# Delta-rule attention and a GELU MLP on one Trainium2 core: exponent activations parted, a join moved, unread products in other banks, masks earlier on GpSimd

## The chip, the cores and the metric

The kernel runs on one core of a Trainium2 chip. A core has five engines with a queue each, and each works through its own queue in order: TensorE (PE, with its weight loads shown as PEld), VectorE (DVE), ScalarE (ACT), GpSimd (POOL) and SyncE (SP, which here only starts transfers). They wait for one another through semaphores. The metric is the device time of one execution in microseconds (us), the median of several runs. A profiled execution also gives a trace, with the start and duration of every instruction; its times are those quoted below.

## The reference

Two parts, all in fp32. The first is attention by the delta rule, for 4 batches, 8 heads, 768 steps and a head size of 48; a 48x48 state is carried from step to step:

```python
k_n = k / (np.linalg.norm(k, axis=-1, keepdims=True) + 1e-06)
for t in range(S):
    kt, vt, bt = (k_n[:, :, t], v[:, :, t], beta[:, :, t, None])
    y[:, :, t] = np.einsum('bhd,bhde->bhe', q[:, :, t], state)
    v_old = np.einsum('bhde,bhd->bhe', state, kt)
    state = state + bt[:, :, :, None] * np.einsum('bhd,bhe->bhde', kt, vt - v_old)
```

Its result, with the heads side by side, is a matrix x of 3072 tokens by 384, which goes through a layer with GELU:

```python
h = x @ w_in                               # 384 -> 2048
g = 0.5 * h * (1.0 + erf(h * inv_sqrt2))
out = g @ w_out                            # 2048 -> 384
```

The weights w_in and w_out reach the chip as 64-bit floating-point words and are turned into fp32 there.

## The kernel before

**Tiling.** The 768 steps are cut into 12 chunks of 64, and the recurrence within a chunk becomes a triangular system that is solved at once. A unit is one chunk of a pair of batches, one batch on each half of the 128 partitions; there are two pairs, so two units to a chunk. Four units (chunks 0 and 1) form `first`: first[0], first[1] are chunk 0 (first[:NA], NA=2), first[2], first[3] are chunk 1.

**The triangular solve.** For a group of two chunks the systems are inverted in blocks of 32x32 by elimination (`eliminate_steps`): for each row j, one product into tmp (L558) and one sum into Nu (L560). In groups 0 and 1 these run on DVE, in later ones on GpSimd. The first group's rows are followed by ng, a factor made from the norms (L1344), and by two transpositions, Nu to XM (L569) and Nu to Zf (L572). Then the blocks are joined by products on TensorE. For chunk 0, `join_first(0)` does so by products psJ (L634), scaled into XM by DVE (L643) and ScalarE (L647), after GpSimd has scaled a block (L625); `join_first(1)` issues the second set (L634) and copies psJ on (L649). For chunk 1 it is `join`, whose level 0 ends in DVE products into XM (L613) and whose level 1 ends in copies on ScalarE (L617). `upper_left` makes two copies on ScalarE, one for each half (L586). `masked` multiplies the unit's products P by a triangular mask on GpSimd (L506); P is copied out of PSUM by ScalarE (L503). `scale_v` multiplies V by its norms on GpSimd (L421). `against_state` multiplies V of chunk 0 by ng, for first[0] on GpSimd (L783) and for first[1] on ScalarE, a head at a time (L780, 8 of them).

**The weights' decoding.** There are eight parts of w_in (`n` from 0 to 7) and then the parts of w_out. `fetch` starts a part's transfer on SP; `begin` takes the exponent bits out on DVE (L265 or L268); `exponents` turns them into a scale on ScalarE, by two Prelu for most parts (`two_kinks`; the calls are recorded at L1073 because they go through `keep`, which holds program order) or by one Relu (L271); `mantissas` makes the significand on DVE (L286, then L289); `signed` multiplies the two on DVE (L297, for some parts L296 before it) and then calls `fetch(n + 4)`, since the buffer of part n is free from there on.

**The layer.** Chunks 0 and 1 go through it by plain products, `fc1` (L976, with a GELU on ScalarE for each, recorded at L1073) and `fc2` (L991); from chunk 2 on it is by a scheme with seven products for eight (L1024, L1090).

**What sets the order.** Up to `by_hand.close()` the order of every engine's queue is that of the program, written out by hand. `unread` issues products of a blank tile whose results nobody reads; they go to the two PSUM banks of `sq`, which are used for other products too. `behind_rows` makes a step's first TensorE instruction wait for the latest DVE instruction in program order; `between` and `idle` say which steps follow which row. After that, `plan` is a list of steps with due times in units of a chunk, sorted by `emit`; DVE and GpSimd keep that order, and so do the calls of ScalarE and SP that go through `keep`. `decode_in` gives the due times of parts 3 to 7, and `behind_vector` makes a GpSimd step wait for the latest DVE instruction.

Of the kernel before, what the change touches and what calls it, by code (L numbers as in the profile page):

```python
# [8 lines left out]
F32 = mybir.dt.float32  # L9
U32 = mybir.dt.uint32  # L10
I32 = mybir.dt.int32
I16 = mybir.dt.int16
# [7 lines left out]
def kernel(  # L20
# [54 lines left out]
    def sq(name, *shape):  # L75
        return small[0].tile([128, *shape], F32, tag="sq", name=name)
# [179 lines left out]
    def high(e, dt):  # L256

        return e.bitcast(dt).rearrange("q (n w) -> q n w", w=2)[:, :, 1]
# [9 lines left out]
            nc.vector.tensor_scalar(e, raw[:, :, 1], 20, 0x7FF, op0=ALU.logical_shift_right,  # L268
                                    op1=ALU.bitwise_and)

    def exponents(n, put=lambda fn, *args, **kw: fn(*args, **kw)):  # L271
        e = halves[n][3]
        if two_kinks(n):
            f = e.bitcast(F32)
            put(nc.scalar.activation, f, e.bitcast(I32), ACT.Prelu, bias=lim[:, 2:3], scale=1.0,
                alpha=FLAT)
            put(nc.scalar.activation, high(e, I16), f, ACT.Prelu, bias=lim[:, 3:4], scale=128.0,
                alpha=1.0 / FLAT)
        else:
            put(nc.scalar.activation, e, e, ACT.Relu, bias=lim[:, 0:1], scale=float(2 ** 23))  # L280

# [33 lines left out]

    def decode_in():

        marks = {3: (None, 1.079, 0.99, 1.08), 4: (1.0, 1.113, 1.1, 1.13),
                 5: (1.12, 1.18, 1.14, 1.2), 6: (1.19, 1.24, 1.21, 1.25),
                 7: (1.245, 1.3, 1.29, 1.36)}  # L320
        steps = []
        for n, (a, b, c, d) in marks.items():
            if a is not None:
                steps += [(a, (begin, n))]
            steps += [(b, (exponents, n, keep)), (c, (mantissas, n)), (d, (signed, n))]
        return steps

    NW = len(w_parts)
# [176 lines left out]
    def masked(u, engine=nc.gpsimd):  # L505
        engine.tensor_tensor(u.P, u.P, mask_h, op=ALU.mult)  # L506
# [76 lines left out]
        steps += [(0.1, diagonal)]  # L583
        return steps + [(1.9, back, x) for x in range(3 if g else 2)]

    def upper_left(us, put=lambda fn, *args: fn(*args)):  # L586

        for p in range(2):
            top = slice(p * C, p * C + HB)
            put(nc.scalar.copy, Zf[0][top, us, 0:HB], Zf[0][top, us, HB:C])  # L590

# [178 lines left out]

    SIDES = [(0, 0), (1, 0), (0, 1), (1, 1)]

    def against_state(us):

        for u in us:
            u.W = u.V
            u.y = None
            if u.c == 0 and u.a:
                for h in range(H):
                    nc.scalar.mul(u.V[:, h], u.V[:, h], ng[:, u.a, h:h + 1])  # L780
                continue
            if u.c == 0:
                nc.gpsimd.tensor_tensor(u.W, u.V,  # L783
                                        ng[:, u.a].unsqueeze(2).to_broadcast([128, H, D]),
                                        op=ALU.mult)
                continue
            w = D if u.c == 1 else D + C
            psK = dn("psK")
            u.psK = psK[:, :, 0:NP * w].rearrange("q r (j d) -> q r j d", d=w)
            for j in range(NP):  # L790
                for r, p in QUADS:
                    rows = slice(r * C, r * C + D)
                    nc.tensor.matmul(u.psK[HALF[p], r, j, :], lhsT=u.Kt[rows, p, j, :],  # L793
                                     rhs=SQ[rows, u.a, p ^ r, j, 0:w], start=True, stop=True)
            if u.c == 1:
                u.psQ = psK[:, :, NP * D:2 * NP * D].rearrange("q r (j d) -> q r j d", d=D)
                against_queries([u])
        if us[0].c > 2:
            subtract(us)
# [438 lines left out]
    def at(first, last, steps):  # L1238

        total, done, timed = sum(s[0] for s in steps), 0.0, []  # L1240
        for w, *step in steps:
            timed.append((first + (last - first) * (done + 0.5 * w) / total, step))
            done += w
        return timed
# [11 lines left out]
            src = psB[HALF[p]].rearrange("q c (a p h) -> q c a p h", p=2, h=H)[:, :, :, p, :]  # L1256
            nc.scalar.mul(beta_m[HALF[p], c0:c1], src, -1.0)

    def unread(*cols):

        psI = sq("psI", 512)
        for n in cols:
            m = min(n, 128)
            nc.tensor.matmul(psI[0:m, 0:n], lhsT=blank[:, 0:m], rhs=blank[:, 0:n],
                             start=True, stop=True)
# [17 lines left out]
    n0 = wk.tile([128, 2 * NA, H], F32, tag="n0", name="n0", bufs=1)  # L1283
    for c in range(2):
        ns[c] = n0[:, c * NA:(c + 1) * NA]
    unread(512, 512)
    for u in first:
        squares(u, n0[:, u.t], nc.gpsimd if u.t == 1 else nc.vector)
        transposed(u, (0,))
# [27 lines left out]
    def latest(engine):  # L1317
        return next(i for i in reversed(nc.cur_bb.bb.instructions) if i.engine == engine)

    def behind_rows(fn, *args, engine=mybir.EngineType.PE):  # L1320

        after = latest(mybir.EngineType.DVE)
        n = len(nc.cur_bb.bb.instructions)
        fn(*args)
        new = next(i for i in nc.cur_bb.bb.instructions[n:] if i.engine == engine)
        tc.add_manual_dep(new, after.name,
                          mybir.DependencyInfo(mybir.DependencyClass.Sync,
                                               mybir.DependencyReason.DATA), reason="time")

    def turned(us, x):  # L1330
        for u in us:
            transposed(u, (x,))

    between = {9: [(turned, third, 0)], 10: [(grams, third)], 12: [(turned, third, 1)],
               15: [(turned, fourth, 0)], 17: [(grams, fourth)]}
    idle = {14: (256,), 18: (256,), 19: (256,), 20: (256,), 21: (256,), 22: (256,), 23: (256,), 24: (256,), 25: (256,), 28: (256,)}
    between.update({j: [(unread, *cols)] for j, cols in idle.items()})
    for fn, *args in rows:
        fn(*args)
        for step in between.get(args[0], ()) if args else ():  # L1340
# [1 line left out]
    for x in sums_:  # L1342
        sum_of_squares(*x)
    nc.vector.scalar_tensor_tensor(ng, gms[0][:, 0:NA], -1.0, ns[0], ALU.mult, ALU.mult)  # L1344
    behind_rows(unread, 512, 512)
    back0[0](*back0[1:])
    against_state(first[:NA])
    for u in first[:NA]:
        masked(u)
    back1[0](*back1[1:])  # L1350
    join_first(0)
    upper_left(slice(0, NA * H))
    after = latest(mybir.EngineType.PE)
    for n in range(n_in, n_in + 2):
# [3 lines left out]
                               if i.engine == mybir.EngineType.SP), after.name,  # L1358
                          mybir.DependencyInfo(mybir.DependencyClass.Sync,
                                               mybir.DependencyReason.DATA), reason="time")  # L1360
    unread(512, 256)
    begin(0)
    mantissas(0, (0,))
    join_first(1)
# [39 lines left out]
            steps = steps[:-1] + [(turn, tiles[c, a]) for a in range(NA)]  # L1404
        return [(t, step) for t, step in zip(times, steps) if t is not None]

    def behind_vector(fn, *args):
        behind_rows(fn, *args, engine=mybir.EngineType.Pool)

    plan = [at(c + 1 + 0.25 * (c == 1), c + 2 + 0.25 * (c == 0), ffn_steps(c)) for c in range(4)]  # L1410
    plan += [at(c + 1, c + 3, ffn_steps(c)) for c in range(4, NC, 2)]
    plan += [decode_in(), at(1.365, 1.9, decode_steps(n_in, NW)), at(1.91, 1.911, [(1.0, late)])]
    rows1, join1 = eliminate_steps(1), join_steps(1)
    plan += [at(1.1, 1.105, [(1.0, load, 3)]),
             at(1.112, 1.1121, [(1.0, upper_left, slice(NA * H, NU), keep)]),
             [(t, (together, (join, 0, range(NA, 2 * NA), level))) for level, t in enumerate((1.085, 1.16))],
]
    sums = [(1.0, sum_of_squares, tiles[3, a], h) for a in range(NA) for h in range(H)]
    plan += [at(1.48, 1.8, sums), at(1.81, 1.811, [(1.0, fn, c) for c in (2, 3) for fn in (norms, prep)]), at(1.9, 1.905, [(1.0, finish_both)]),
             *[at(t, t + 0.001, [(1.0, behind_vector, fn, u)]) for t, fn, u in (  # L1420
                 (1.201, scale_v, first[2]), (1.231, scale_v, first[3]),
                 (1.322, masked, first[2]), (1.37, masked, first[3]))],
             at(1.31, 1.311, [(1.0, together, (against_state, first[NA:]))]),
             at(1.325, 1.326, [(1.0, subtract, first[NA:])]),
             at(1.42, 1.421, [(1.0, together, (solve, first[NA:], ()))]),
# [144 lines left out]
```

## Time and profile before

| what | value |
|---|---|
| time, median of 3 runs | 621.89 us (621.54 to 622.21) |
| the profiled execution's own time | 623.14 us |
| its span | 621.4 us |
| mean granted clock of TensorE | 0.992 |
| PE busy | 606.9 us, 98% |
| DVE busy | 438.2 us, 71% |
| ACT busy | 246.2 us, 40% |
| POOL busy | 215.0 us, 35% |

The span runs from the first to the last recorded instruction; the execution's own time has what lies around it besides. Busy shares are means over the whole span. In the page's 40 slices (15.5 us each, tenths busy) the front differs from the rest:

```profile
PE   7899999999999999999999999999999999999997
DVE  7989999999867697765859656859646946422532
ACT  5777777624532265134452034452033322044200
POOL 6020232000479721786222885222885200000000
PEclk9889999999999999999999999999999999999999
```

TensorE's share includes the unread products of the first four slices. GpSimd is idle through most of the second and the fourth slice. PEclk is the clock that TensorE was granted, in tenths of full speed.

### The profile page before, as it was taken

To read this page: it belongs to the slowest core of one execution; us is meant where nothing else is said; L and a number is where in the kernel's file an instruction comes from. 1 tells how busy PE (TensorE), PEld (TensorE's weight loads), DVE (VectorE), ACT (ScalarE), POOL (GpSimd) and SP (SyncE) were. 2 spreads that over 40 slices of the span, in tenths; PEclk is the share of its full clock that TensorE was granted. 3 is DMA by queue.
4 is the path that set the end of the run, shared out by engine and by line. 5 is a ranking of instruction groups with operands and counts; after the bars stand their busy time and mean duration, and the time that the engine had idled before them with its cause. 6 is when DMAs were issued, how large, how long until landed. Compare 5 with 4: busy or idle time off the path is not lost.

```text
span 621.4 us, 19448 instructions
## 1 busy us (share of the span) xinstructions
PE 606.9 (98%) x8204; PEld 535.1 (86%) x8204; DVE 438.2 (71%) x806; ACT 246.2 (40%) x559; POOL 215.0 (35%) x323
## 2 busy tenths in 40 slices
PE   7899999999999999999999999999999999999997
PEld 5757766776899998998899998899998899988997
DVE  7989999999867697765859656859646946422532
ACT  5777777624532265134452034452033322044200
POOL 6020232000479721786222885222885200000000
PEclk9889999999999999999999999999999999999999
DMA  9687855102433443453033433023421001000011
GB/s 133 130 245 250 177 154 129 25 1 46 70 38 55 71 90 42 65 109 40 10 50 62 87 70 39 9 40 48 81 44 18 11 2 27 7 20 1 0 27 25
DMA packets 159574, 39.60 MB, mean 64 GB/s; under 512 B 151168, under 2 KB 154368, under 8 KB 159488
## 3 DMA queue, kind: packets, MB, share of 16 engines
q1 hardware_dynamic: 156816, 37.34, 31.1%
q10 hardware_dynamic: 2672, 1.03, 0.9%
q8 instruction: 64, 1.05, 0.7%
q14 instruction: 22, 0.18, 0.1%
HBM read 33.62 MB, written 4.72 MB: 62 GB/s over the span
## 4 chain that ended last, share of the span: by engine, by line
PE 80%; DVE 13%; ACT 2%; issue 2%; DMA 1%; SPq 0%; POOL 0%; DVEq 0%; ACTq 0%; POOLq 0%
PE psX L1024 12%; PE psY L1090 11%; PE psY L1024 9%; PE psX L1090 9%; PE psV L1090 6%; PE psZ L1090 6%; PE psV L1024 4%; PE psZ L1024 4%; DVE Nu L560 3%; DVE tmp L558 3%; PE psK L793 3%; PE psO L991 3%; PE psQ L813 2%; PE psY L883 2%; PE psG L459 2%
## 5 line engine op out<-in xcount | busy, mean ns | idle before, releaser
L394 POOL TENSOR_TENSOR n<-n,half 128x16 f32<-128x16 f32 x10 | 31.3, 3125 | 150.5 <-DVE n L392 130.2
L560 POOL TENSOR_TENSOR Nu<-Nu,tmp 128x30 f32<-128x30 f32 (+14 forms) x120 | 65.2, 544 | 9.4
L558 POOL TENSOR_TENSOR tmp<-Nu 128x30 f32<-128x30 f32 (+14 forms) x120 | 62.2, 518 | 9.4
L1090 PE MATMUL psX<-xT,w_in_sb 128*128 128x256 f32 (+1 forms) x288 | 62.6, 346 | 0.0
L1024 PE MATMUL psX<-w_out_sb,G 128*128 128x192 f32 x320 | 56.1, 329 | 0.0
L1024 PEld LDWEIGHTS psX<-w_out_sb,G 128*128 128x128 f32 x320 | 52.1, 190 | 0.8
L1090 PEld LDWEIGHTS psX<-xT,w_in_sb 128*128 128x128 f32 x288 | 47.9, 190 | 5.4
L976 PE MATMUL psH<-xT,w_in_sb 128*128 128x256 f32 x192 | 45.3, 386 | 2.3 <-ACT G L1073 1.9
L976 PEld LDWEIGHTS psH<-xT,w_in_sb 128*128 128x128 f32 x192 | 35.4, 190 | 10.5 <-ACT G L1073 5.1
L991 PE MATMUL psO<-w_out_sb,G 128*128 128x384 f32 x128 | 43.9, 490 | 0.0
L912 DVE TENSOR_TENSOR V<-psY,y 64x192 f32<-64x192 f32 (+1 forms) x60 | 21.3, 355 | 30.3 <-PE psY L895 26.3
L1118 DVE TENSOR_TENSOR psY<-psY,pu 128x512 f32<-128x512 f32 x20 | 14.0, 699 | 40.2 <-PE psY L1090 40.2
L1090 PE MATMUL psY<-xT,w_in_sb 128*128 128x256 f32 (+1 forms) x192 | 41.5, 345 | 0.0
L1073 ACT COPY xT<-psX 128x768 f32<-128x768 f32 x9 | 7.2, 798 | 79.5 <-PE psX L953 79.5
L1073 ACT COPY pu<-psZ 128x512 f32<-128x512 f32 x40 | 23.4, 586 | 37.4 <-PE psZ L1090 35.0
L991 PEld LDWEIGHTS psO<-w_out_sb,G 128*128 128x128 f32 x128 | 23.6, 190 | 14.1
L1090 PEld LDWEIGHTS psY<-xT,w_in_sb 128*128 128x128 f32 x192 | 32.1, 191 | 3.5
L1073 ACT ACTIVATE G<-G 128x512 f32<-128x512 f32 x40 | 25.2, 631 | 21.0 <-DVE G L1126 20.8
L1073 ACT ACTIVATE G<-psY 128x512 f32<-128x512 f32 x20 | 11.9, 596 | 45.3 <-PE psY L1090 45.3
L1126 DVE TENSOR_TENSOR G<-psY,pu 128x512 f32<-128x512 f32 x20 | 13.8, 688 | 22.2 <-PE psY L1090 21.5
L1024 PE MATMUL psY<-w_out_sb,G 128*128 128x192 f32 x160 | 28.1, 329 | 0.0
L1024 PE MATMUL psZ<-T,pu 128*128 128x192 f32 x160 | 28.1, 329 | 0.0
(236 smaller groups left out, 1381.2 us busy)
## 6 DMA issues: line engine op xcount, KB each, us to landing
Kp<-in_k_dram SPq DMA_DIRECT2D x76, 96.0 KB, 3.1
w_out_sb<-in_moe_w_in_dram SPq DMA_DIRECT2D x24, 256.0 KB, 4.6
V<-in_v_dram SPq DMA_DIRECT2D x48, 96.0 KB, 3.2
w_raw<-in_moe_w_out_dram SPq DMA_DIRECT2D x12, 384.0 KB, 4.0
out_dram<-o_sb SPq DMA_DIRECT2D x40, 96.0 KB, 2.2
Qp<-in_k_dram SPq DMA_DIRECT2D x64, 32.0 KB, 2.1
G<-in_moe_w_out_dram SPq DMA_DIRECT2D x4, 384.0 KB, 4.3
Qp<-in_q_dram SPq DMA_DIRECT2D x96, 16.0 KB, 2.0
```

Of the source, the lines that this page charges most:

```text
L394: nc.gpsimd.tensor_tensor(flat, flat, half, op=ALU.pow)
L558: rows_on.tensor_tensor(tmp, nu[:, j + 1:, j:j + 1].to_broadcast([128, n, j]), nu[:, j:j + 1, 0:j].to_broadcast([128, n, j]), op=ALU.mult)
L560: rows_on.tensor_tensor(nu[:, j + 1:, 0:j], nu[:, j + 1:, 0:j], tmp, op=ALU.add)
L793: nc.tensor.matmul(u.psK[HALF[p], r, j, :], lhsT=u.Kt[rows, p, j, :], rhs=SQ[rows, u.a, p ^ r, j, 0:w], start=True, stop=True)
L912: nc.vector.tensor_tensor(dst, src, pairs(u.y[at_], s), op=ALU.add)
L976: nc.tensor.matmul(psH, lhsT=w_in_sb[:, f // 2, m, f % 2 * 128:(f % 2 + 1) * 128], rhs=xTs[c][:, m, :], start=(m == 0), stop=(m == NM - 1))
L991: nc.tensor.matmul(u.psO, lhsT=G[:, u.a, f, :], rhs=w_out_sb[:, f, :], start=(f == 0), stop=(f == NF - 1))
L1024: nc.tensor.matmul(ps_, lhsT=lhs[:, f, :], rhs=rhs[:, f, :], start=first and f == 0, stop=f == FH - 1, skip_group_check=not first)
L1073: i = fn(*args, **kw)
L1090: nc.tensor.matmul(ps_[:, i], lhsT=lhs[:, f // 2, f % 2 * 128:(f % 2 + 1) * 128], rhs=rhs, start=first and i == 0, stop=True, skip_group_c ...
L1118: nc.vector.tensor_tensor(L1["Y1"], L1["Y1"], L1["pu"][:, 0], op=ALU.add)
L1126: nc.vector.tensor_tensor(half(1, 1), shaped(L1["Y1"]), shaped(L1["pu"][:, 0]), op=ALU.add)
```

## The change

Four things, in the diff's order.

1. The two Prelu of a part's exponents become two steps with due times of their own for parts 3 to 7 (`part`, `b0`, `b1`), and the due times of `mantissas` and `signed` move with them. In the resulting order ScalarE has one GELU between the two Prelu of each pair, and DVE has XM's two products of the join ahead of the product of `signed(3)`. `fetch(7)`, which `signed(3)` starts, comes behind the ten loads of chunk 3 on SP. `upper_left` for chunk 1 is parted likewise, its second copy and the join's level 1 fall due a little later, and one Relu (L271) trades places with a GELU.
2. `against_state` for chunk 0 runs wholly on ScalarE: first[0] first, the first four heads of first[1] behind it, its last four heads behind the first join's copies.
3. Unread products go to the layer's PSUM banks (tag "mlp") where they stand between rows (`filled`) and at the start; other rows have them, in other sizes, and one of 512 columns in place of two follows ng.
4. On GpSimd the masks of first[0], first[1] and first[2] come ahead of the first join's product, the mask of first[3] and both `scale_v` behind it; `behind_vector` and its four steps in the plan are gone.

```diff
@@ -268,14 +268,16 @@
             nc.vector.tensor_scalar(e, raw[:, :, 1], 20, 0x7FF, op0=ALU.logical_shift_right,
                                     op1=ALU.bitwise_and)
 
-    def exponents(n, put=lambda fn, *args, **kw: fn(*args, **kw)):
+    def exponents(n, put=lambda fn, *args, **kw: fn(*args, **kw), part=(0, 1)):
         e = halves[n][3]
         if two_kinks(n):
             f = e.bitcast(F32)
-            put(nc.scalar.activation, f, e.bitcast(I32), ACT.Prelu, bias=lim[:, 2:3], scale=1.0,
-                alpha=FLAT)
-            put(nc.scalar.activation, high(e, I16), f, ACT.Prelu, bias=lim[:, 3:4], scale=128.0,
-                alpha=1.0 / FLAT)
+            if 0 in part:
+                put(nc.scalar.activation, f, e.bitcast(I32), ACT.Prelu, bias=lim[:, 2:3], scale=1.0,
+                    alpha=FLAT)
+            if 1 in part:
+                put(nc.scalar.activation, high(e, I16), f, ACT.Prelu, bias=lim[:, 3:4], scale=128.0,
+                    alpha=1.0 / FLAT)
         else:
             put(nc.scalar.activation, e, e, ACT.Relu, bias=lim[:, 0:1], scale=float(2 ** 23))
 
@@ -315,14 +317,15 @@
 
     def decode_in():
 
-        marks = {3: (None, 1.079, 0.99, 1.08), 4: (1.0, 1.113, 1.1, 1.13),
-                 5: (1.12, 1.18, 1.14, 1.2), 6: (1.19, 1.24, 1.21, 1.25),
-                 7: (1.245, 1.3, 1.29, 1.36)}
+        marks = {3: (None, 1.079, 1.11, 0.99, 1.1105), 4: (1.0, 1.14, 1.17015, 1.112, 1.172),
+                 5: (1.165, 1.201, 1.232, 1.18, 1.233), 6: (1.225, 1.263, 1.294, 1.24, 1.295),
+                 7: (1.285, 1.325, 1.356, 1.296, 1.357)}
         steps = []
-        for n, (a, b, c, d) in marks.items():
+        for n, (a, b0, b1, c, d) in marks.items():
             if a is not None:
                 steps += [(a, (begin, n))]
-            steps += [(b, (exponents, n, keep)), (c, (mantissas, n)), (d, (signed, n))]
+            steps += [(b, (exponents, n, keep, (i,))) for i, b in enumerate((b0, b1))]
+            steps += [(c, (mantissas, n)), (d, (signed, n))]
         return steps
 
     NW = len(w_parts)
@@ -583,9 +586,9 @@
         steps += [(0.1, diagonal)]
         return steps + [(1.9, back, x) for x in range(3 if g else 2)]
 
-    def upper_left(us, put=lambda fn, *args: fn(*args)):
-
-        for p in range(2):
+    def upper_left(us, put=lambda fn, *args: fn(*args), part=(0, 1)):
+
+        for p in part:
             top = slice(p * C, p * C + HB)
             put(nc.scalar.copy, Zf[0][top, us, 0:HB], Zf[0][top, us, HB:C])
 
@@ -770,19 +773,14 @@
 
     SIDES = [(0, 0), (1, 0), (0, 1), (1, 1)]
 
-    def against_state(us):
+    def against_state(us, heads_=range(H)):
 
         for u in us:
             u.W = u.V
             u.y = None
-            if u.c == 0 and u.a:
-                for h in range(H):
+            if u.c == 0:
+                for h in heads_:
                     nc.scalar.mul(u.V[:, h], u.V[:, h], ng[:, u.a, h:h + 1])
-                continue
-            if u.c == 0:
-                nc.gpsimd.tensor_tensor(u.W, u.V,
-                                        ng[:, u.a].unsqueeze(2).to_broadcast([128, H, D]),
-                                        op=ALU.mult)
                 continue
             w = D if u.c == 1 else D + C
             psK = dn("psK")
@@ -1256,9 +1254,9 @@
             src = psB[HALF[p]].rearrange("q c (a p h) -> q c a p h", p=2, h=H)[:, :, :, p, :]
             nc.scalar.mul(beta_m[HALF[p], c0:c1], src, -1.0)
 
-    def unread(*cols):
-
-        psI = sq("psI", 512)
+    def unread(*cols, tag="sq"):
+
+        psI = (small[0] if tag == "sq" else ps).tile([128, 512], F32, tag=tag, name="psI")
         for n in cols:
             m = min(n, 128)
             nc.tensor.matmul(psI[0:m, 0:n], lhsT=blank[:, 0:m], rhs=blank[:, 0:n],
@@ -1283,7 +1281,7 @@
     n0 = wk.tile([128, 2 * NA, H], F32, tag="n0", name="n0", bufs=1)
     for c in range(2):
         ns[c] = n0[:, c * NA:(c + 1) * NA]
-    unread(512, 512)
+    unread(512, 512, tag="mlp")
     for u in first:
         squares(u, n0[:, u.t], nc.gpsimd if u.t == 1 else nc.vector)
         transposed(u, (0,))
@@ -1317,12 +1315,12 @@
     def latest(engine):
         return next(i for i in reversed(nc.cur_bb.bb.instructions) if i.engine == engine)
 
-    def behind_rows(fn, *args, engine=mybir.EngineType.PE):
+    def behind_rows(fn, *args):
 
         after = latest(mybir.EngineType.DVE)
         n = len(nc.cur_bb.bb.instructions)
         fn(*args)
-        new = next(i for i in nc.cur_bb.bb.instructions[n:] if i.engine == engine)
+        new = next(i for i in nc.cur_bb.bb.instructions[n:] if i.engine == mybir.EngineType.PE)
         tc.add_manual_dep(new, after.name,
                           mybir.DependencyInfo(mybir.DependencyClass.Sync,
                                                mybir.DependencyReason.DATA), reason="time")
@@ -1331,10 +1329,14 @@
         for u in us:
             transposed(u, (x,))
 
+    def filled(*cols):
+        unread(*cols, tag="mlp")
+
     between = {9: [(turned, third, 0)], 10: [(grams, third)], 12: [(turned, third, 1)],
                15: [(turned, fourth, 0)], 17: [(grams, fourth)]}
-    idle = {14: (256,), 18: (256,), 19: (256,), 20: (256,), 21: (256,), 22: (256,), 23: (256,), 24: (256,), 25: (256,), 28: (256,)}
-    between.update({j: [(unread, *cols)] for j, cols in idle.items()})
+    idle = {13: (512,), 14: (256,), 18: (256,), 19: (256,), 20: (512,), 22: (512,), 24: (512,),
+            26: (512,), 28: (512,), 30: (512,)}
+    between.update({j: [(filled, *cols)] for j, cols in idle.items()})
     for fn, *args in rows:
         fn(*args)
         for step in between.get(args[0], ()) if args else ():
@@ -1342,13 +1344,18 @@
     for x in sums_:
         sum_of_squares(*x)
     nc.vector.scalar_tensor_tensor(ng, gms[0][:, 0:NA], -1.0, ns[0], ALU.mult, ALU.mult)
-    behind_rows(unread, 512, 512)
+    behind_rows(filled, 512)
     back0[0](*back0[1:])
-    against_state(first[:NA])
-    for u in first[:NA]:
+    against_state(first[:1])
+    against_state(first[1:NA], range(H // 2))
+    for u in first[:3]:
         masked(u)
     back1[0](*back1[1:])
     join_first(0)
+    masked(first[3])
+    for u in first[NA:]:
+        scale_v(u)
+    against_state(first[1:NA], range(H // 2, H))
     upper_left(slice(0, NA * H))
     after = latest(mybir.EngineType.PE)
     for n in range(n_in, n_in + 2):
@@ -1358,7 +1365,7 @@
                                if i.engine == mybir.EngineType.SP), after.name,
                           mybir.DependencyInfo(mybir.DependencyClass.Sync,
                                                mybir.DependencyReason.DATA), reason="time")
-    unread(512, 256)
+    unread(512, 512)
     begin(0)
     mantissas(0, (0,))
     join_first(1)
@@ -1404,22 +1411,17 @@
             steps = steps[:-1] + [(turn, tiles[c, a]) for a in range(NA)]
         return [(t, step) for t, step in zip(times, steps) if t is not None]
 
-    def behind_vector(fn, *args):
-        behind_rows(fn, *args, engine=mybir.EngineType.Pool)
-
     plan = [at(c + 1 + 0.25 * (c == 1), c + 2 + 0.25 * (c == 0), ffn_steps(c)) for c in range(4)]
     plan += [at(c + 1, c + 3, ffn_steps(c)) for c in range(4, NC, 2)]
     plan += [decode_in(), at(1.365, 1.9, decode_steps(n_in, NW)), at(1.91, 1.911, [(1.0, late)])]
     rows1, join1 = eliminate_steps(1), join_steps(1)
     plan += [at(1.1, 1.105, [(1.0, load, 3)]),
-             at(1.112, 1.1121, [(1.0, upper_left, slice(NA * H, NU), keep)]),
-             [(t, (together, (join, 0, range(NA, 2 * NA), level))) for level, t in enumerate((1.085, 1.16))],
+             *[at(t, t + 0.0001, [(1.0, upper_left, slice(NA * H, NU), keep, (p,))])
+               for p, t in enumerate((1.111, 1.17))],
+             [(t, (together, (join, 0, range(NA, 2 * NA), level))) for level, t in enumerate((1.085, 1.1703))],
 ]
     sums = [(1.0, sum_of_squares, tiles[3, a], h) for a in range(NA) for h in range(H)]
     plan += [at(1.48, 1.8, sums), at(1.81, 1.811, [(1.0, fn, c) for c in (2, 3) for fn in (norms, prep)]), at(1.9, 1.905, [(1.0, finish_both)]),
-             *[at(t, t + 0.001, [(1.0, behind_vector, fn, u)]) for t, fn, u in (
-                 (1.201, scale_v, first[2]), (1.231, scale_v, first[3]),
-                 (1.322, masked, first[2]), (1.37, masked, first[3]))],
              at(1.31, 1.311, [(1.0, together, (against_state, first[NA:]))]),
              at(1.325, 1.326, [(1.0, subtract, first[NA:])]),
              at(1.42, 1.421, [(1.0, together, (solve, first[NA:], ()))]),
```

## The prediction

> **What bounds the kernel now.** First I read the page's chain of work that ended last:
>
> ```profile
> PE 80%; DVE 13%; ACT 2%; issue 2%; DMA 1%; SPq 0%; POOL 0%; DVEq 0%; ACTq 0%; POOLq 0%
> ```
>
> TensorE holds four fifths; VectorE's 13% (81 us of 621.4) lies almost wholly in the first 60 us, so there DVE's queue sets the end. The change touches just that front and the decoding of weights up to 86 us. From 86 us TensorE has only short stops (0.29 us at 102 us and 0.35 at 135 us are the longest I found), so what the first 86 us gain or lose I carry to the end one for one.
>
> Second, the timeline of the front (columns: start, duration, engine, line, operation, tiles, count, and in brackets the idle time before and its releaser):
>
> ```profile
> 18.28 0.59 ACT L503 COPY P<-psG 128x512 f32<-128x512 f32 x1 [0.36 <-PE psG L459]
> 19.00 0.32 DVE L560 TENSOR_TENSOR Nu<-Nu,tmp 128x150 f32<-128x150 f32 x1
> 37.69 2.09 DVE L569 STREAM_TRANSPOSE XM<-Nu 128x1024 f32<-128x1024 f32 x1
> 37.82 0.83 POOL L783 TENSOR_TENSOR V<-V,ng 128x384 f32<-128x384 f32 x1 [21.14 <-DVE ng L1344]
> 37.84 3.23 PE L1264 MATMUL psI<-G 128*128 128x512 f32 x4 [0.22 <-DVE ng L1344]
> 38.61 2.52 POOL L506 TENSOR_TENSOR P<-P,mask 128x512 f32<-128x512 f32 x2
> 39.66 1.93 DVE L572 STREAM_TRANSPOSE Zf<-Nu 128x1024 f32<-128x1024 f32 x1
> 41.00 1.49 PE L634 MATMUL psJ<-XM,G 32*64 32x64 f32 x32
> 41.73 1.04 POOL L625 TENSOR_TENSOR G<-Zf,gm 32x512 f32<-32x512 f32 x1 [0.61 <-DVE Zf L572]
> 42.52 0.84 DVE L643 TENSOR_TENSOR XM<-psJ,gm 32x256 f32<-32x256 f32 x2 [0.92 <-PE psJ L634]
> 46.09 0.96 DVE L289 SCALAR_TENSOR_TENSOR w_in_sb<-w_out_sb,w_in_sb 128x768 f32<-128x768 uint32 x1
> ```
>
> The rows of elimination (L558, L560) run on DVE back to back until 37.55 and the transpositions L569, L572 follow; no other engine delays them. GpSimd has idled for 21.14 us when ng lets L783 go, and its two masks (L506) come behind L783, beside the transpositions. The first join product (L634) could start when L569 ends, near 39.78, but TensorE is in unread products until 41.07.
>
> Third, the timeline of the decoding stage, engines beside one another:
>
> ```profile
> 59.68 1.66 SPq L1073 DMA_DIRECT2D w_out_sb<-in_moe_w_in_dram  x3
> 65.61 2.12 ACT L1073 ACTIVATE w_e<-w_e,lim 128x768 f32<-128x768 int32 x2
> 67.59 0.62 ACT L1073 ACTIVATE G<-psH 128x256 f32<-128x256 f32 x2
> 68.00 2.86 PE L976 MATMUL psH<-xT,w_in_sb 128*128 128x256 f32 x12 [0.67 <-ACT G L1073]
> 68.85 1.02 POOL L421 TENSOR_TENSOR V<-V,n 128x384 f32<-128x384 f32 x1 [26.08 <-DMA Qp<-in_q_dram]
> 69.23 1.47 DVE L289 SCALAR_TENSOR_TENSOR w_in_sb<-w_out_sb,w_in_sb 128x768 f32<-128x768 uint32 x1
> 70.62 0.55 DVE L265 TENSOR_SCALAR w_e<-w_out_sb 128x768 int32<-128x768 int32 x1
> 77.91 1.47 POOL L506 TENSOR_TENSOR P<-P,mask 128x512 f32<-128x512 f32 x1 [2.37 <-DVE w_e L268]
> 78.27 1.92 DVE L289 SCALAR_TENSOR_TENSOR w_out_sb<-w_raw,w_out_sb 128x768 f32<-128x768 uint32 x1
> 82.04 1.56 PE L976 MATMUL psH<-xT,w_in_sb 128*128 128x256 f32 x6 [1.22 <-ACT G L1073]
> ```
>
> A pair of exponents (two Prelu, 2.12 us) holds the GELUs behind it, and TensorE waits 0.67. And L289, 0.96 alone, takes 1.47 and 1.92 beside a GpSimd product: each time it ends about 0.82 us after that product, as if it could only then stream. The same holds of L297 (71.09, 1.58 against 0.95) with the second L421. Transpositions (L569: 2.09 beside L783 and a mask, 2.10 alone) and products with one operand in PSUM are not lengthened.
>
> **Masks freed into the elimination.** L783 was what made GpSimd wait for ng. It goes to ScalarE (8 more L780, 0.24 each, 1.9 us; they end near 40.7, before the join's copies need ScalarE at 41.6, so I cost them at nothing; bare, 1.9). With it goes the only wait for DVE ahead of the masks: in the changed code they wait for the copies of P (ended 18.87, 20.07, 21.27 by the rows of L503) and a memset ended at 16.68. So three masks run in 18.9 to 23.3 us, among the rows, not beside the transpositions. Rows read two SBUF tiles, as L289 does. What of a DVE product lay beside the rest of a GpSimd one: L289 lost 0.51 of 0.64 (68.85+1.02−69.23), L297 0.63 of 0.76, L289 0.96 of 1.11, so all but some 0.14. A mask alone is 1.26 (2.52/2). Row by row, with mask 1 from 18.95, mask 2 at the next gap and mask 3 behind that, the row L560 (150 elements) ends 1.1 later, the next product 2.1, and the one behind mask 3 3.1: I take 3.1, some 1.03 a mask. Bounds: 0, if short rows pass between; 4.4 (3x1.47, the mask of 77.91). For passing: a 128x128 sum of L1055 lost only 0.20 and 0.27 beside GpSimd, but beside its short elimination rows. I keep near the locked end, since L1160 (0.69 alone) took 2.85 beside one long GpSimd product. Behind the rows queue both transpositions, the joins and weight decoding, all on DVE: nothing covers the 3.1.
>
> The Trainium skill's page GPSIMD Engine Reference, section 1 Specifications, lists SBUF interfaces shared with VectorE, contended by DVE instructions with two SBUF inputs or in a 2-port performance mode. The rows above agree for two inputs; for the mode no run here shows a one-input product that starts inside a GpSimd one. Were L268 and L286 of part 0 caught so, they would lie under mask 4 near 42.8 to 43.7: an estimate by that page's rule is +0.2, so 624.1 in place of 623.9.
>
> **The join, −0.43.** One unread 512 in place of two behind ng, in the "mlp" banks, frees TensorE before 39.78; L634 then starts 39.85 and ends by 41.35 even at 1.49. L643 follows L572 at 41.6 in place of 42.52; the second product waits for L625 (ends 42.8): 42.87 in place of 43.90, and all behind it 1.03 earlier. But behind L625 GpSimd now has mask 4 (1.26) and two scale_v (0.83 each), 42.8 to 45.8, and L289, at 45.05, would lie 0.75 under the last: 0.6 lost. Net 0.43 (bounds 0 and 1.05). With the 3.1 the stage behind starts 2.7 later. The other unread products follow rows that set the pace and are read by nobody; cover gone, one 512 is about 0.8 (3.23/4). The granted clock was half in 38.37 to 41.78 and I leave it so: L634's 1.49 is from there, and it ends before L572.
>
> **Decoding, −0.65.** TensorE's stops in 52 to 86 us, from the timeline: 0.23, 0.28, 0.51 (join waits for XM), 0.20, 0.23, 0.84 (GELUs behind the pair; 0.67 by the row's label), 1.38 (1.22 by the label of 82.04: a GELU behind an exponent that waits for L268, which queues behind the L289 that the mask held): 3.7 in all. Parting the pairs puts one GELU between the two Prelu of parts 3 to 7; XM's two products go ahead of signed(3); masks and scale_v leave, and that exponent goes behind its GELU. DVE gets 0.51+0.63+0.31 (L833)+0.96 = 2.4 back. Against it, signed(5) waits 0.55 to 0.9 for its second, later Prelu. I put the sum at −1.85 with weights in time. They are not: fetch(7) hangs on signed(3), which moves behind the ten loads of chunk 3 on SP (4 Qp, 2 Kp, 4 Qp). The ten loads leave 1.7 us earlier for it; their first user, a sum of squares on Kp, starts at 85.62, so that gains nothing. Its three 256 KB issues leave SP near 67.8 to 69.0 in place of 59.7 to 61.3 and land, at the 2.8 to 3.3 us that such loads take when few others run, by 71.4 to 71.9; L265 for part 7 would else start near 70.2. So DVE idles 1.0 to 1.8, mean 1.25 after what slack signed(6) leaves, and 1.85−1.25 = 0.6 to 0.65 stays. Bounds: +0.9 lost (latest landing, no shelter) and −1.85 (load in time).
>
> **Sum.** 3.1 − 0.43 − 0.65 = +2.0. On the profiled execution (621.4 span, 623.14 with what lies around it, 1.25 above the median of the runs, 621.89) that is 625.1; on the median, which I predict, 623.9.
>
> **Rivals.** (1) Rows half caught: masks lie in the gaps and two of three rows' losses are those of L1055; D about 1.5, sum +0.4, 622.3. For it: short rows, 0.3 us. Against: every L289-like case lost nearly all. (2) The faster side: masks cost rows nothing, because the lock needs a long DVE stream. Place: rows j=6 to 9. Then −1.08: 620.8; with fetch(7) in time too, −2.3: 619.6. Not slower than before holds up to D of 1.08; faster by 0.2% needs D near 0 and the load in time. Against it: no row shows a two-SBUF product of 384 or more that passes a GpSimd product. (3) Heavier: masks at 1.47 each (4.4), or weights of part 7 landing past 73: +3.3, 625.2.
>
> **How the numbers follow.** Forecast 0.57, own range 623.0 to 624.9; rival 1 0.13; rival 2 0.06 at 620.8 and 0.13 at 619.6; rival 3 0.11. A change below 0.2% (1.24 us) can't be told from none by such measurements. Slower by more (over 623.13): 0.51 of the forecast's 0.57, and rival 3: 0.62. Within: 0.06 of the forecast, 0.11 of rival 1, 0.03 of rival 2: 0.20. Faster: 0.13+0.03+0.02 = 0.18. The range, 620.0 to 625.5, leaves out most of the best case and the tail of rival 3.
>
> **What would show it.** L509 (the masks) at 19 to 23 us, and rows of L561/L563 beside them 1 us long or more: forecast; masks there and rows at 0.3: rival 2. ng near 40.6. L637's first product right behind L572, no longer 0.9 after it. L289's successor beside scale_v at 1.5. DVE idle before part 7's begin, releaser a w_out_sb load, and no GELU wait over 0.4 at TensorE before it. The masks running at 38 to 42 us would make the prediction wrong outright.

## The result, and the profile after

| | us |
|---|---|
| before, median of 4 runs | 621.81 (621.54 to 622.21) |
| after, median of 4 runs | 628.88 (628.42 to 629.65) |
| after by before | 1.0114, 95% interval 1.0097 to 1.0132 |
| profiled execution after: time, span, mean clock | 628.51, 626.8, 0.992 |

The change costs 7.1 us; 623.9 was forecast. The direction was right, the time lies outside the range. Three stretches of the timeline after answer to those shown of before (columns as there). First the front:

```profile
19.14 4.18 POOL L509 TENSOR_TENSOR P<-P,mask 128x512 f32<-128x512 f32 x3 [2.69 <-ACT P L506]
19.49 1.29 DVE L563 TENSOR_TENSOR Nu<-Nu,tmp 128x168 f32<-128x168 f32 x1
20.81 1.39 DVE L561 TENSOR_TENSOR tmp<-Nu 128x184 f32<-128x184 f32 x1
22.23 1.30 DVE L563 TENSOR_TENSOR Nu<-Nu,tmp 128x184 f32<-128x184 f32 x1
23.56 0.37 DVE L561 TENSOR_TENSOR tmp<-Nu 128x198 f32<-128x198 f32 x1
40.39 2.09 DVE L572 STREAM_TRANSPOSE XM<-Nu 128x1024 f32<-128x1024 f32 x1
```

Three masks run at 19.1 to 23.3 us among the rows of elimination, as the waits said, not beside the transposition at 40.39. Three rows take 1.29, 1.39 and 1.30 where the profile before has 0.33 to 0.35 for such rows, as here:

```profile
20.09 0.35 DVE L558 TENSOR_TENSOR tmp<-Nu 128x184 f32<-128x184 f32 x1
```

Next, what lies behind the first join:

```profile
44.33 0.84 DVE L646 TENSOR_TENSOR XM<-psJ,gm 32x256 f32<-32x256 f32 x2
45.56 1.47 POOL L509 TENSOR_TENSOR P<-P,mask 128x512 f32<-128x512 f32 x1
45.82 1.62 DVE L288 TENSOR_SCALAR w_in_sb<-w_out_sb 128x768 uint32<-128x768 uint32 x1
46.98 1.93 POOL L424 TENSOR_TENSOR V<-V,n 128x384 f32<-128x384 f32 x2
48.38 1.34 DVE L291 SCALAR_TENSOR_TENSOR w_in_sb<-w_out_sb,w_in_sb 128x768 f32<-128x768 uint32 x1
```

L646 follows the second transposition at once (that ends 44.29), in place of 0.92 after it. But L288, with one input, started inside the fourth mask and took 1.62; L291 took 1.34 for 0.96 beside a scaling. In the profile before the same product (L286 there) took 0.55:

```profile
43.87 0.55 DVE L286 TENSOR_SCALAR w_in_sb<-w_out_sb 128x768 uint32<-128x768 uint32 x1
```

The third is the decoding of part 7:

```profile
71.48 2.45 SPq L1071 DMA_DIRECT2D w_out_sb<-in_moe_w_in_dram  x3
72.11 0.96 DVE L291 SCALAR_TENSOR_TENSOR w_in_sb<-w_out_sb,w_in_sb 128x768 f32<-128x768 uint32 x1
77.36 0.56 DVE L265 TENSOR_SCALAR w_e<-w_out_sb 128x768 int32<-128x768 int32 x1 [4.29 <-DMA w_out_sb<-in_moe_w_in_dram]
78.94 2.83 PE L974 MATMUL psH<-xT,w_in_sb 128*128 128x256 f32 x12 [2.75 <-ACT w_e L1071]
84.88 1.56 PE L974 MATMUL psH<-xT,w_in_sb 128*128 128x256 f32 x6 [1.89 <-ACT G L1071]
```

fetch(7) leaves SP at 71.48 to 73.93; VectorE, free at 73.07, waits 4.29 us for it, and TensorE stops for 2.75 and 1.89 behind that.

### The profile page after: what moved, and what is told of

Read it like the earlier page. It is cut to its first block, busy times and chain, and to the rows that moved or that the text cites. A ratio compares the mean times of both kernels' runs of the same rounds, so it can differ in the third digit from the quotient of the medians.

```text
span 626.8 us, 19444 instructions
## 1 busy us (share of the span) xinstructions
PE 608.3 (97%) x8202; PEld 535.0 (85%) x8202; DVE 440.2 (70%) x806; ACT 247.7 (40%) x567; POOL 214.4 (34%) x322
## 3 DMA queue, kind: packets, MB, share of 16 engines
q10 hardware_dynamic: 2672, 1.03, 0.9%
## 4 chain that ended last, share of the span: by engine, by line
PE 78%; DVE 14%; ACT 3%; issue 2%; DMA 2%; POOL 0%; SPq 0%; DVEq 0%; ACTq 0%; POOLq 0%
PE psX L1022 12%; PE psY L1088 11%; PE psY L1022 9%; PE psX L1088 9%; PE psV L1088 6%; PE psZ L1088 6%; PE psV L1022 4%; PE psZ L1022 4%; DVE Nu L563 3%; DVE tmp L561 3%; PE psK L791 3%; PE psO L989 3%; PE psY L881 2%; PE psQ L811 2%; PE psG L462 2%
## 5 line engine op out<-in xcount | busy, mean ns | idle before, releaser
L1022 PE MATMUL psX<-T,G 128*128 128x192 f32 x160 | 27.6, 326 | 0.6 <-issue 0.6
```

Source lines behind the costliest of these rows:

```text
L1022: nc.tensor.matmul(ps_, lhsT=lhs[:, f, :], rhs=rhs[:, f, :], start=first and f == 0, stop=f == FH - 1, skip_group_check=not first)
```

## The experiments

To compare the kernels, each profile is cut at three starts: ng (the elimination ends), the first fc1 product (psH; the decoding stage begins) and the first fc2 product (psO; it ends). The columns are those starts' differences in us, from rows of the traces:

| profile | ng starts | ng to psH | psH to psO | psO to the end | span |
|---|---|---|---|---|---|
| before, as recorded | 37.55 | 14.57 | 33.43 | 535.88 | 621.4 |
| b0_before_again | 37.14 | 14.26 | 33.22 | 535.88 | 620.5 |
| after | 40.25 | 14.46 | 35.66 | 536.43 | 626.8 |
| e1_masks_held | 37.11 | 14.50 | 36.72 | 536.22 | 624.6 |
| e2_weights_ahead | 40.18 | 14.49 | 31.27 | 536.21 | 622.1 |
| e3_held_and_ahead | 37.19 | 16.08 | 31.28 | 536.73 | 621.3 |
| e7_last_products_away | 37.49 | 13.51 | 31.88 | 536.65 | 619.5 |
| e9_unread_as_before | 37.00 | 13.91 | 31.86 | 535.93 | 618.7 |
| e9_again | 37.14 | 14.43 | 31.88 | 535.91 | 619.4 |
| e11_three_beside_psum | 36.98 | 13.94 | 31.18 | 535.94 | 618.0 |
| x1_changed_unread_before | 40.40 | 14.47 | 35.40 | 535.91 | 626.2 |
| x2_pairs_whole | 37.10 | 13.41 | 32.50 | 535.88 | 618.9 |
| e4_before_masks_free | 39.08 | 14.27 | 33.07 | 535.88 | 622.3 |
| e5_before_weights_late | 37.80 | 15.20 | 35.95 | 535.92 | 624.9 |

**Masks held.** In the changed kernel GpSimd's first mask gets a wait for ng; the other two queue behind it.

```diff
+    on_ng = latest(mybir.EngineType.DVE)
     behind_rows(filled, 512)
...
+    m = len(nc.cur_bb.bb.instructions)
     for u in first[:3]:
         masked(u)
+    tc.add_manual_dep(next(i for i in nc.cur_bb.bb.instructions[m:]
+                           if i.engine == mybir.EngineType.Pool), on_ng.name,
+                      mybir.DependencyInfo(mybir.DependencyClass.Sync,
+                                           mybir.DependencyReason.DATA), reason="time")
```

> The changed kernel, but GpSimd's first mask waits for ng, so that three masks run from about 37.9 us beside the two transpositions. Theory (masks among the elimination rows cost about 2.9 us, and late weights of part 7 the rest): ng back near 37.5, the stage behind about 2.7 earlier, 626.2 us. Rival (the front is longer because of the unread products in the layer's banks or ScalarE's longer list): ng moves back but the stage does not, 628 or more.

Measured: 626.04 us, 1.0068 of before (1.0053 to 1.0083), 2.84 less than the change. Its timeline beside ng:

```profile
37.11 0.14 DVE L1346 SCALAR_TENSOR_TENSOR ng<-gm,n 128x16 f32<-128x16 f32 x1
37.25 2.11 DVE L572 STREAM_TRANSPOSE XM<-Nu 128x1024 f32<-128x1024 f32 x1
37.42 3.76 POOL L509 TENSOR_TENSOR P<-P,mask 128x512 f32<-128x512 f32 x3 [21.19 <-DVE ng L1346]
```

Three masks lie over the transposition, which takes 2.11 as always. The theory holds for the front. The time gains less than the front: psH to psO grows by 1.06. Most of it is VectorE's wait for the weights of part 7, 5.23 us in place of 4.29: they do not come as much earlier as their user does. The granted clock was also half from 76.0 to 82.8 us in this profile; how much of the small rest is from that is not told apart.

**Weights ahead.** The ten loads of chunk 3 fall due behind signed(3).

```diff
-    plan += [at(1.1, 1.105, [(1.0, load, 3)]),
+    plan += [at(1.1106, 1.1107, [(1.0, load, 3)]),
```

> The changed kernel, but the ten loads of chunk 3 fall due behind signed(3), so that fetch(7) leaves SP ahead of eight of them, as before the change. Theory: VectorE's 4.29 us without work ahead of part 7 goes, TensorE's stops of 2.9 and 2.1 go with it, 624.8 us (range 624 to 626). Rival (the parted pairs' own waits cost the time behind 55 us): at most 1 us back, 628.

Measured: 623.86 us, 1.0033 (1.0019 to 1.0048), 5.0 less than the change, more than expected. Its timeline at the place shown above:

```profile
70.59 0.96 DVE L299 SCALAR_TENSOR_TENSOR w_in_sb<-w_in_sb,w_e 128x768 f32<-128x768 f32 x1 [0.65 <-ACT w_e L1071]
72.94 0.55 DVE L265 TENSOR_SCALAR w_e<-w_out_sb 128x768 int32<-128x768 int32 x1
73.27 5.45 PE L974 MATMUL psH<-xT,w_in_sb 128*128 128x256 f32 x24
80.44 1.56 PE L974 MATMUL psH<-xT,w_in_sb 128*128 128x256 f32 x6 [0.64 <-ACT G L1071]
```

L265 follows L291 with no wait. The 0.65 in front of L299 is VectorE's wait for the second, later Prelu of a parted pair.

**Each cause alone in the kernel before.** In the first kernel V of first[0] goes to ScalarE, which frees two masks; in the second the loads of chunk 3 fall due ahead of signed(3).

```diff
-            if u.c == 0 and u.a:
+            if u.c == 0:
                 for h in range(H):
                     nc.scalar.mul(u.V[:, h], u.V[:, h], ng[:, u.a, h:h + 1])
                 continue
-            if u.c == 0:
-                nc.gpsimd.tensor_tensor(u.W, u.V,
-                                        ng[:, u.a].unsqueeze(2).to_broadcast([128, H, D]),
-                                        op=ALU.mult)
-                continue
```

```diff
-    plan += [at(1.1, 1.105, [(1.0, load, 3)]),
+    plan += [at(1.0798, 1.0799, [(1.0, load, 3)]),
```

> The kernel before with one edit: first[0]'s V is multiplied by ng on ScalarE, so two masks on GpSimd no longer wait for VectorE. Theory: each costs the rows 0.98 us, about +2.0, 623.8 us, with ng near 39.5. Rival (rows pass the masks, the loss is elsewhere): ng stays near 37.5 and the time near 621.8.

> The kernel before with one edit: the ten loads of chunk 3 fall due ahead of signed(3), so fetch(7) leaves SP behind them. Theory: the weights of part 7 land some 4 us after VectorE is free for them, and 2 to 3.5 us of it reach the end, 624.7 us. Rival (as the prediction put it, an idle 1.0 to 1.8): at most 623.3.

Measured: 624.03 (1.0036, 1.0023 to 1.0049) and 625.34 (1.0056, 1.0038 to 1.0075), against 621.98 for the kernel before in the same set. The second kernel's profiled run, 626.60, is the slowest of its four. The first one's timeline among the rows:

```profile
18.08 1.27 POOL L506 TENSOR_TENSOR P<-P,mask 128x512 f32<-128x512 f32 x1 [1.92 <-ACT P L503]
18.11 1.41 DVE L558 TENSOR_TENSOR tmp<-Nu 128x150 f32<-128x150 f32 x1
19.56 0.32 DVE L560 TENSOR_TENSOR Nu<-Nu,tmp 128x150 f32<-128x150 f32 x1
19.73 1.27 POOL L506 TENSOR_TENSOR P<-P,mask 128x512 f32<-128x512 f32 x1 [0.38 <-ACT P L503]
19.91 1.29 DVE L558 TENSOR_TENSOR tmp<-Nu 128x168 f32<-128x168 f32 x1
```

The two masks lengthen the rows that they meet by 1.09 and 0.96 us. From the first row to ng the elimination takes 21.25 us with no mask beside it, 23.31 with two, 24.17 with three. In the second kernel the same wait of VectorE appears, and TensorE's stop behind it:

```profile
74.65 0.56 DVE L265 TENSOR_SCALAR w_e<-w_out_sb 128x768 int32<-128x768 int32 x1 [3.02 <-DMA w_out_sb<-in_moe_w_in_dram]
78.40 2.86 PE L976 MATMUL psH<-xT,w_in_sb 128*128 128x256 f32 x12 [1.81 <-ACT G L1073]
```

**Both undone, then the last GpSimd products moved.** The first kernel has both edits. In the second the fourth mask and both scale_v leave the stretch behind the join; `behind_vector` is that of the kernel before.

```diff
...
-    masked(first[3])
-    for u in first[NA:]:
-        scale_v(u)
...
+    behind_vector(masked, first[3])
     for u in first[:NA]:
         next_state(u)
...
+    plan += [at(1.0848, 1.0849, [(1.0, behind_vector, scale_v, first[2])]),
+             at(1.2258, 1.2259, [(1.0, behind_vector, scale_v, first[3])])]
```

> The changed kernel with both edits: masks held for ng and fetch(7) ahead of the chunk's loads. Theory (the two causes are apart and together hold the whole loss): 628.88 less 2.84 less 5.02, 621.0 us, a little under the kernel before. Rival (one lateness hid part of the other): 622 or more.

> As e3_held_and_ahead, and the fourth mask and both scale_v leave the stretch behind the first join: the mask goes beside the sums L900, the scalings beside L616 and beside VectorE's wait for signed(5). Theory (in that stretch they lengthen L268 by 0.15, L288 by 1.07 and L291 by 0.39, which eats the join's gain): L288 back to 0.55, the stage behind some 0.9 to 1.1 earlier, 620.1 us. Rival (one-input L288 was late for another reason, or the stretch has slack): 621.0.

Measured: 621.19 (0.9991, 0.998 to 1.0001) and 621.14 (0.9991, 0.9977 to 1.0004). With both causes undone the loss is gone. Of the second kernel, the trace bears out the mechanism but the median does not show the gain. In its timeline L288 is back at 0.55, and psH starts 13.51 behind ng in place of 14.50 (e1's figure, the same front with the three products in it):

```profile
42.49 0.70 DVE L268 TENSOR_SCALAR w_e<-w_out_sb 128x768 uint32<-128x768 uint32 x1
43.12 0.55 DVE L288 TENSOR_SCALAR w_in_sb<-w_out_sb 128x768 uint32<-128x768 uint32 x1
45.08 0.96 DVE L291 SCALAR_TENSOR_TENSOR w_in_sb<-w_out_sb,w_in_sb 128x768 f32<-128x768 uint32 x1
```

L268 keeps its 0.70, so that part was not the mask's: it starts inside L628 of GpSimd. The moved products give 0.6 of the gain back between psH and psO (31.88 for 31.28). The front of the first kernel, 16.08 (in a profiled run of 623.01, its slowest), is longer for another reason, seen in its windows (stretch, its length, then busy time and count of PE, PEld, DVE, ACT and POOL, the granted clock, and the share and rate of the DMA):

```profile
13.00:31.00 18.00, 17.21 (x293) 14.91 (x294) 16.35 (x42) 9.08 (x18) 3.23 (x3) 0.53 0.63 132
```

and in its timeline:

```profile
34.54 7.14 PE L1262 MATMUL psI<-G 128*128 128x256 f32 x18
42.79 0.84 DVE L646 TENSOR_TENSOR XM<-psJ,gm 32x256 f32<-32x256 f32 x2 [1.51 <-PE psJ L637]
```

The granted clock was 0.53 from 13 to 31 us (0.83 in the recorded profile of before), TensorE fell behind the rows, worked through its unread products until 41.68, and the join's product, ready to start at 39.4, waited. In 3 of that kernel's 11 runs and 4 of e7's 12 the mean clock was 0.986 and the time 622.4 to 623.5.

**Unread products as before.** The changed kernel's unread products are replaced by those of the kernel before, first in e7, then in the changed kernel itself.

```diff
...
-    idle = {13: (512,), 14: (256,), 18: (256,), 19: (256,), 20: (512,), 22: (512,), 24: (512,),
-            26: (512,), 28: (512,), 30: (512,)}
-    between.update({j: [(filled, *cols)] for j, cols in idle.items()})
+    idle = {14: (256,), 18: (256,), 19: (256,), 20: (256,), 21: (256,), 22: (256,), 23: (256,), 24: (256,), 25: (256,), 28: (256,)}
+    between.update({j: [(unread, *cols)] for j, cols in idle.items()})
...
-    behind_rows(filled, 512)
+    behind_rows(unread, 512, 512)
...
```

> As e7_last_products_away, but the unread products, their sizes, places and banks are those of the kernel before. Theory (one unread 512 in place of two is what starts the join product 0.9 to 1.0 earlier): that gain goes, 621.0 us. Rival (the unread products don't matter): 620.1.

> The changed kernel, but its unread products are those of the kernel before (sizes, places, banks, two 512 behind ng). Theory after e9 (the new unread products buy the join nothing, and cost some 0.5 us behind 86 us): 628.3 us, with the fourth of the change's parts a small loss. Rival (they start the join 0.9 earlier, as the prediction had it): 629.8.

> The kernel before, unchanged, for a second profile beside these: its recorded profile was 1.25 us over the median of its runs. Theory (that execution started its elimination late): span near 620.2, with ng near 37.0 rather than 37.55. Rival (the excess lies behind the front): ng at 37.55.

Measured: e9 620.24 (0.9967, 0.9955 to 0.998), against its expectation: faster than e7, not slower. x1 627.95 (1.0087, 1.0073 to 1.01), 0.9 less than the change. So the new unread products look like a small loss; within each pair the intervals overlap a little, but the traces show a part of it behind psO (below). Nor are they needed to start the join: L646 stands 0.03 behind the transposition in e7 and in e9. The second profile of the kernel before says why the gain looked larger than it is:

```profile
41.58 0.41 DVE L643 TENSOR_TENSOR XM<-psJ,gm 32x256 f32<-32x256 f32 x1 [0.36 <-PE psJ L634]
```

There the wait is 0.36, not 0.92; in that execution the granted clock was full from 37 to 42 us, where it was half from 38.4 to 41.8 in the recorded profile. ng came at 37.14, nearly as expected, and the span was 620.5, so the recorded profile of before had 0.4 of bad luck ahead of ng and 0.3 in the join.

**Pairs whole.** e9 with whole exponent pairs and the due times of the kernel before in `decode_in`, `upper_left`, the join and the loads (the two diffs of the change there, taken back).

> As e9_unread_as_before, but the exponent pairs are whole again, and XM's products, upper_left, the join's level 1 and the loads of chunk 3 have the due times of the kernel before; the masks and scale_v stay where they are in e9. Theory (parting the pairs and putting XM's products ahead is worth 0.8 us by itself, what is left of 2.0 is GpSimd's products leaving VectorE): 621.0 us, with a GELU wait of about 0.7 back at TensorE behind a whole pair. Rival (all of it is GpSimd's products): 620.3.

Measured: 621.34 (0.9989, 0.9978 to 1.0). TensorE's wait is back:

```profile
66.95 2.86 PE L973 MATMUL psH<-xT,w_in_sb 128*128 128x256 f32 x12 [0.68 <-ACT G L1070]
```

psH to psO is 32.50 against 31.86 in e9: 0.64 for the pairs and XM's place, 0.7 of before's 33.22 for the moved GpSimd products.

**The best version, again and once more moved.** The kernel of e9 a second time, and one with both scale_v beside L616 and the fourth mask beside L824.

```diff
...
-    behind_vector(masked, first[3])
...
-             at(1.2258, 1.2259, [(1.0, behind_vector, scale_v, first[3])])]
+             at(1.08491, 1.08492, [(1.0, scale_v, first[3])]),
+             at(1.3095, 1.3096, [(1.0, behind_vector, masked, first[3])])]
```

> The kernel of e9_unread_as_before again, since its five runs lay closer together than those of its neighbours. Theory (it is faster than the kernel before by its earlier joins and by the decoding): 620.2 us, 0.25% under the kernel before. Rival (those five runs happened on a favourable phase of TensorE's clock): 621 or more, spread to 623.

> As e9_unread_as_before, with both scale_v beside L616 and the fourth mask beside L824, which read PSUM. Theory (in e9 the mask still lengthens L299 from 0.96 to 1.41 and the second scaling another L299 to 1.27; beside reads of PSUM they cost at most 0.3 in all): 619.9 us. Rival (VectorE's last 0.5 us there lie under TensorE's own work): 620.2.

Measured: 620.67 (0.9979, 0.9964 to 0.9995) and 620.10 (0.9979, 0.9961 to 0.9997; 12 runs from 619.73, two of them above 623 at a clock of 0.983 and less). So the kernel of e9 is faster than the kernel before in both sets, by 0.3% and 0.2%, and e11's median is the lowest; e11 is not told from e9 by the intervals. The rival named for e9_again is in part right: one of its 12 runs took 625.26 at a clock of 0.981, and in its profile the join waited where it did not in e9:

```profile
41.70 0.85 DVE L646 TENSOR_TENSOR XM<-psJ,gm 32x256 f32<-32x256 f32 x2 [0.44 <-PE psJ L637]
```

In e11's timeline the three products lie beside reads of PSUM and cost VectorE 0.13 and 0.34 (L299 1.09 for 0.96, L831 1.36 for 1.02):

```profile
58.55 1.41 DVE L616 TENSOR_TENSOR XM<-psJ,gm 32x512 f32<-32x512 f32 x2
58.66 1.62 POOL L424 TENSOR_TENSOR V<-V,n 128x384 f32<-128x384 f32 x2 [16.43 <-DVE w_e L265]
60.00 1.09 DVE L299 SCALAR_TENSOR_TENSOR w_in_sb<-w_in_sb,w_e 128x768 f32<-128x768 f32 x1
71.66 1.02 DVE L824 TENSOR_TENSOR V<-psK,V 128x384 f32<-128x384 f32 x2
71.77 1.28 POOL L509 TENSOR_TENSOR P<-P,mask 128x512 f32<-128x512 f32 x1 [11.50 <-DVE w_in_sb L291]
72.60 1.36 DVE L831 TENSOR_TENSOR V<-V,gm 128x384 f32<-128x384 f32 x2
```

## Why the prediction was wrong, step by step

Against b0_before_again the span grew by 6.3 us; the median of the kernel before lies 0.33 below that profile's time, and the changed kernel's 0.37 above its own profile's, which makes the 7.0. The terms:

| step | forecast | measured in the traces |
|---|---|---|
| masks among the rows | +3.1 | +2.93 (24.17 less 21.24) |
| join and what lies behind it, ng to psH | −0.43 | +0.20 (14.46 less 14.26) |
| decoding, psH to psO | −0.65 | +2.44 (35.66 less 33.22) |
| psO to the end | 0 | +0.55 (536.43 less 535.88) |
| start of the rows | 0 | +0.19 (16.08 for 15.89; it varies from 15.7 to 16.6 over the profiles) |

**Masks: right, in place, kind and size.** One mask cost the row that it met 0.95 to 1.09; 1.03 was forecast. e1 and e4 show it from both sides. That a row of 0.3 us could pass or be half caught, rivals 2 and 1, is refuted. One ground was misread, though: that no row shows a large product with two SBUF inputs passing a GpSimd product. The profile before has one, beside the power that GpSimd computes for the norms (L394):

```profile
79.34 3.73 POOL L394 TENSOR_TENSOR n<-n,half 128x16 f32<-128x16 f32 x1
80.61 0.95 DVE L296 SCALAR_TENSOR_TENSOR w_e<-w_raw,w_e 128x768 uint32<-128x768 uint32 x1
```

So not every GpSimd instruction holds VectorE; in these traces the masks, the scalings and L628 do.

**Decoding: the mechanism was right, the size of one of its terms, the late fetch(7), was not; this is the step that failed.** With weights in time I forecast −1.85; e2 has −1.95. The late fetch(7) was put at 1.25 and cost 4.39 (35.66 less 31.27). VectorE was free when forecast (73.07 in the trace; 70.2 plus the front's 2.7 makes 72.9). The weights were to be there at 71.4 to 71.9 in before's time, 74.1 to 74.6 in after's, and L265 started at 77.36. Of those 2.8 to 3.3 us, 2.2 were on SP: the last issue ended at 73.93, not at 71.7 (69.0 plus 2.7). SP's queue ahead of it:

```profile
60.39 2.29 SPq L105 DMA_DIRECT2D Kp<-in_k_dram  x2
62.73 3.85 SPq L124 DMA_DIRECT2D Qp<-in_q_dram  x4
67.45 1.28 SPq L105 DMA_DIRECT2D Kp<-in_k_dram  x2
68.78 2.60 SPq L124 DMA_DIRECT2D Qp<-in_q_dram  x4
```

The ten issues took 8.7 us, as in the kernel before (8.6), but began about 0.8 late, as the two of Kp ahead of them took 2.29 for 1.36; and fetch(7)'s own three took 2.45 where 1.2 was forecast. The rest is the landing: the two issues whose landing the trace has landed 3.7 us after they began, and L265 started 4.8 us after the third began. I had taken the 2.8 to 3.3 of a quiet stretch; the same transfer in the kernel before took 6.7 and 7.4. And I deducted some slack, while the stage paid for the whole wait (4.39 for VectorE's 4.29). Rival 3, which named weights of part 7 past 73, was the case that came, but it allowed only 1.3 us beyond the forecast where 3.1 were due.

**The join: half right.** L646 came 0.9 nearer to the transposition, but the shorter unread products can't be credited with it: I had read one profile's wait as a property of the kernel. Over the nine profiles with the old unread products the wait is 0.03 in four, 0.28 to 0.44 in three, 0.92 and 1.07; over the five with the new ones it is 0.03 in four and 1.51 in one. The longest, 1.51 (e3) and 1.07 (e5), go with the longest stretch of half clock (17.1 us, to 30.5 and 31.6). That TensorE's clock sets it is argued from these rows; whether the old products make a wait likelier, fourteen profiles do not settle. And what followed L646 was priced for one locked product of VectorE, L291 at 0.6; L291 lost 0.38, and L288, which I costed at nothing in the sum, lost 1.07. The Trainium skill's page GPSIMD Engine Reference, section 1 Specifications, lists contention with a VectorE instruction in a 2-port mode beside that with two SBUF inputs; I gave it 0.2 in a sentence beside the sum. The trace agrees in that L288, with one SBUF input, took 1.62 inside a mask and 0.55 without one (e7); whether it runs in such a mode no run here shows. Nor was it true that no run showed a one-input product starting inside a GpSimd one: L268 did at 80.11 in the profile before, inside L394, and took 0.57. The three products together cost the front 0.99 (14.50 less 13.51); how much of it is L288's own was not parted.

**After 86 us: not quite one for one.** All nine profiles with the old unread products have 535.88 to 535.94 from psO to the end, and the five with the new ones 536.21 to 536.73. The difference sits in one stop of TensorE near 260 us:

```profile
262.85 2.76 PE L1022 MATMUL psX<-T,G 128*128 128x192 f32 x16 [0.62 <-issue]
```

The label "issue" is a wait for nothing that the profile shows. It is 0.32 to 0.90 in the five profiles with the new unread products and absent from the nine others, x1's among them, so that edit brings it; how is open. Two readings behind the one-for-one were wrong without harm. Of VectorE's part of the chain only 30 us lie in the first 60 us, and 29 between 105 and 136 us, in the second group's rows. And TensorE's longest stop behind 86 us is not 0.35 but 0.69 in that profile:

```profile
248.28 1.76 PE L793 MATMUL psK<-SQ,Kt 48*64 48x112 f32 x64 [0.69 <-DVE SQ L902]
```

The time from psO to the end stayed within 0.06 us over the nine all the same.

**ScalarE's 8 more products at nothing: right.** In e4 ng to psH is 14.27, as in b0.

## What to carry to other kernels

A wait that looks like a nuisance may be what keeps a GpSimd product out of a VectorE chain; when an edit removes it, ask where in time that engine will now run, and what VectorE does there: rows that read two SBUF tiles lost here, and so did L288 with one. When a transfer's issue moves behind others on a queue, build its landing from the queue: each earlier issue's wait, and latencies measured under the traffic that will be there; the time until it lands, not the time until it is issued, is the price. And before pricing a wait from one profile, take a second one and compare TensorE's granted clock: here that took the wait from 0.92 to 0.36 in the same kernel, and from 0.03 to 0.44 in e9's.

## What the runs showed that I had not expected

A one-input uint32 product of VectorE, started inside a mask, took 1.62 us for 0.55 (in after, e1, e2 and x1 alike), and L268, started inside L628, 0.70 for 0.56; both ended 0.41 to 0.42 after the GpSimd product. Those that had started before a GpSimd product did were not lengthened (L265 at 70.62 in the profile before: 0.55), nor was L268 inside the power L394. The phase of TensorE's slow stretches is another from execution to execution: the granted clock from 13 to 31 us was 0.53, 0.78, 0.83 and 0.91 in four profiles of kernels with nearly the same work there (e3, b0, before, e7), and fixed unread products meet it differently each time. An earlier stage did not bring its weights as much earlier: with the front 3.1 us shorter in e1, VectorE's wait in the decoding stage grew from 4.29 to 5.23.
